# A fused delta-rule and maxout kernel: the first four pieces in program order on every engine, T1's transposes a link later, and half of T read by ScalarE

## The chip, the cores and the metric

The kernel runs on one core of a Trainium2 chip. The metric is the device time of one execution in microseconds (us). Executions of one kernel scatter by about one per cent to either side: the kernel before took from 586.9 to 599.4 us over 39 runs of one series (runs over 1.5% above the fastest of their kernel count as slow, here seven of the 39). So small differences are judged from series of runs taken on the same chip, and with a 95% interval. Profiled executions are single runs with their own span; where two of them are compared, the text says so.

## The reference, cut to what matters

```python
for t in range(S):                       # 4 batches, 8 heads, S = 768, D = 48
    y[:, :, t] = q_t @ state
    v_old = state.T @ k_t                # k normalised
    state = state + beta_t * outer(k_t, v_t - v_old)
x = y.transpose(0, 2, 1, 3).reshape(B * S, H * D)        # 3072 x 384
h = max(x @ w1, x @ w2, x @ w3)                          # 3072 x 768
out = h @ w_out
```

The kernel turns the recurrence into chunks of 64 tokens. For each chunk a triangular system has to be solved; its solution is called T. Then products with T give the updates, and the chunk's outputs go into the maxout block. In the rows below, names with p_ are products on TensorE: p_h is a piece of the maxout block, p_e, p_f, p_z, p_j and p_u are products with T or its parts, p_k, p_q, p_y and p_s those with the state, for the outputs and for the state's update, p_g the grams (products of keys with keys and queries), p_t and p_x transposes. T1 is a part of T that is needed transposed; VectorE transposes it (rows t<-ut).

## The kernel before: the parts that matter

There are six maxout blocks, numbered 0 to 5 here (the recorded texts call them stages, so the second stage is block 1). Block 0 comes in 31 pieces (the first 18 are 256 columns wide and take TensorE some 1.5 us each at full clock), the others in 22 pieces (2.8 us for each of the first 18). Between the pieces, "links" of the recurrence for the next chunks are emitted, so that TensorE (PE) always has dense products to fill in. A piece's product lies in one of two PSUM buffers; ScalarE (ACT) copies the first of three pieces to h, VectorE (DVE) takes the maximum with the two others.

```python
def ps_ffn(shape, name):
    return psum.tile(shape, FP32, name=name, tag="ffn", bufs=2)
...
    if i == 0:
        nc.scalar.copy(h, p_h)
    else:
        nc.vector.tensor_tensor(out=h, in0=h, in1=p_h, op=ALU.max)
    yield
```

The solve runs on DVE in small steps; its result goes through DRAM, as its layout changes on the way:

```python
def solve(m):
    ...                                   # norms, then 15 or 31 steps of two DVE operations
    for half in range(2):
        nc.sync.dma_start(out=y_d[half]..., in_=y[64 * half : 64 * (half + 1)])
    yield
    for cc in range(2):                   # T of the two chunks: ut[0] and ut[1]
        for half in range(2):
            for bb in range(2):
                (one_queue if m or cc else both_queues)[bb].dma_start(out=ut[cc]..., in_=y_d...)
        yield
```

From block 1 on, all engines run in the order of the program. In block 0 only TensorE does; on the other engines a scheduler orders the instructions when the kernel is built, so that, for instance, steps of a solve can be put ahead of copies that come earlier in the program.

## Time and profile before

| | value |
|---|---|
| median of the first series | 595.75 us (594.52 to 596.13, 3 runs) |
| span of the profiled run | 590.0 us |
| TensorE busy | 540.7 us, 92% |
| VectorE, ScalarE, GpSimd busy | 343.5, 140.6, 119.9 us |
| start of blocks 1 to 5 in the profiled run | 195.1, 277.3, 363.8, 447.7, 523.8 us |

How to read it: TensorE is the bound from 135 us on, so anything there that makes TensorE wait is paid in full. Before that, in the head, TensorE is often idle, and the question is what it waits for. The starts of the blocks cut the run into stretches that can be compared between kernels. The lines that carry this are in the prediction.

### The profile page before, as it was taken

Reading aid. Unit: us, or ns where it says so; the run is one execution under the profiler, and the core shown is the slowest. Engines: PE = TensorE matmul, PEld = TensorE weight load, DVE = VectorE, ACT = ScalarE, POOL = GpSimd, SP = SyncE. Lnnn points to the kernel's source line nnn. Section 1 sums busy time; section 2 is a strip of 40 time slices with the busy share of each in tenths; the row PEclk is TensorE's granted clock in tenths of the full one; section 3 lists DMA queues with packets and bytes.
Section 4 is the critical chain, followed back from the end, with each engine's and each line's share of the span. In section 5 each row is a group of like instructions: output and inputs, shape, how many; then the busy total and the mean of one; then the engine's idle time right before and its main releaser. Section 6 shows DMA issues by size and latency. Waiting matters only on the chain.

```text
span 590.0 us, 18726 instructions
## 1 busy us (share of the span) xinstructions
PE 540.7 (92%) x8106; PEld 319.4 (54%) x8106; DVE 343.5 (58%) x778; ACT 140.6 (24%) x274; POOL 119.9 (20%) x209
## 2 busy tenths in 40 slices
PE   5468477979999999999989999999999999999997
PEld 5337365866556555555545555555455455554443
DVE  1658979387499353799643799563997432201110
ACT  3336645345211222111211121220211111010000
POOL 6024535036400323002803003700001000000000
PEclk9555869999999999999989999999999999999999
DMA  9898985556601554264854454843843201210002
GB/s 158 151 177 232 197 160 131 97 151 129 125 21 28 132 117 96 69 122 94 183 120 82 96 96 109 189 101 67 125 102 75 34 2 54 68 40 1 0 0 53
DMA packets 159505, 58.76 MB, mean 100 GB/s; under 512 B 141184, under 2 KB 153280, under 8 KB 159424
## 3 DMA queue, kind: packets, MB, share of 16 engines
q1 hardware_dynamic: 150736, 51.58, 42.4%
q0 software_dynamic: 3200, 4.82, 3.8%
q10 hardware_dynamic: 5488, 1.18, 1.2%
q8 instruction: 63, 1.03, 0.7%
q14 instruction: 18, 0.15, 0.1%
HBM read 40.21 MB, written 17.30 MB: 97 GB/s over the span
## 4 chain that ended last, share of the span: by engine, by line
PE 81%; DVE 5%; DMA 5%; SPq 3%; issue 3%; ACT 2%; POOL 0%; ACTq 0%; DVEq 0%
PE p_h L823 47%; PE p_o L847 16%; PE p_g L411 4%; PE p_k L676 2%; PE p_u L704 2%; PE p_y L744 2%; PE p_s L726 2%; PE p_q L676 2%; DMA kpad<-in_k_dram 2%; PE p_t L339 1%; SPq L369 1%; PE p_j L659 1%; DMA qpad<-in_q_dram 1%; DMA y_d<-y_bl 1%; PE p_z L646 1%
## 5 line engine op out<-in xcount | busy, mean ns | idle before, releaser
L823 PE MATMUL p_h<-xt,w_sb 128*128 128x512 f32 (+1 forms) x702 | 303.0, 577 | 1.4 <-DVE xt L809 1.4
L823 PEld LDWEIGHTS p_h<-xt,w_sb 128*128 128x128 f32 x702 | 130.0, 194 | 123.5 <-issue 113.3
L833 DVE TENSOR_TENSOR h<-h,p_h 128x512 f32<-128x512 f32 (+1 forms) x78 | 50.2, 644 | 102.6 <-PE p_h L823 102.4
L847 PE MATMUL p_o<-wo_sb,h 128*128 128x384 f32 x288 | 94.6, 487 | 0.0
L847 PEld LDWEIGHTS p_o<-wo_sb,h 128*128 128x128 f32 x288 | 54.2, 190 | 37.2 <-issue 1.0
L277 POOL TENSOR_TENSOR v_t<-v_t,nrm 128x768 f32<-128x768 f32 x12 | 17.8, 1479 | 198.1 <-DVE nrm L250 117.1
L523 DVE TENSOR_TENSOR y_bl<-y_bl,tmp 128x31 f32<-128x31 f32 (+20 forms) x139 | 53.4, 384 | 4.6
L369 POOL DMA_DIRECT2D turned<-in_q_dram x96 | 52.4, 553 | 4.1 <-POOL turned L364 3.1
L519 DVE TENSOR_TENSOR tmp<-x_bl,y_bl 128x31 f32<-128x31 f32 (+20 forms) x139 | 47.2, 340 | 4.0
L411 PE MATMUL p_g<-kqt 48*64 48x64 f32 (+1 forms) x1280 | 34.4, 254 | 13.6 <-ACT kqt L345 5.7
L831 ACT COPY h<-p_h 128x512 f32<-128x512 f32 (+1 forms) x39 | 21.5, 552 | 96.4 <-PE p_h L823 96.4
L411 PEld LDWEIGHTS p_g<-kqt 48*64 48x64 f32 x1280 | 28.8, 151 | 22.7 <-issue 10.3
L855 ACT COPY o_sb<-p_o 128x384 f32<-128x384 f32 x24 | 11.5, 478 | 80.7 <-PE p_o L847 72.5
L428 ACT COPY at<-p_g 128x512 f32<-128x512 f32 x21 | 12.3, 586 | 50.0 <-DVE pt L395 40.0
L238 POOL TENSOR_TENSOR w_sb<-mant,up 128x384 int32<-128x384 int32 x18 | 18.5, 1029 | 16.1 <-DVE mant L234 13.6
L732 DVE TENSOR_TENSOR st<-st,p_s 128x768 f32<-128x768 f32 x11 | 10.4, 950 | 17.5 <-PE p_s L726 17.5
L385 DVE STREAM_TRANSPOSE kqt<-turned 128x256 f32<-128x256 f32 x48 | 17.4, 417 | 5.0 <-DMA turned<-in_k_dram 4.8
L696 ACT COPY qs<-p_q 128x768 f32<-128x768 f32 x11 | 8.8, 798 | 47.6 <-DVE v_t L688 27.6
L215 POOL TENSOR_SCALAR mant<-mant 128x384 f32<-128x384 f32 x24 | 12.7, 531 | 36.3 <-ACT mant L211 36.3
L688 DVE TENSOR_TENSOR v_t<-v_t,p_k 128x768 f32<-128x768 f32 x11 | 10.5, 952 | 15.8 <-PE p_k L676 15.8
L395 DVE TENSOR_TENSOR pt<-p_g,mask 128x512 f32<-128x512 f32 x22 | 15.1, 688 | 6.0 <-PE p_g L411 5.7
L676 PEld LDWEIGHTS p_k<-st,kqt 48*64 48x64 f32 x704 | 12.2, 142 | 10.8 <-issue 10.8
(111 smaller groups left out, 494.7 us busy)
## 6 DMA issues: line engine op xcount, KB each, us to landing
w_bits<-in_moe_w_dram SPq DMA_DIRECT2D x18, 384.0 KB
at_d<-at SPq DMA_DIRECT2D x45, 128.0 KB
v_t<-in_v_dram SPq DMA_DIRECT2D x24, 192.0 KB
turned<-in_q_dram POOLq DMA_DIRECT2D x96, 48.0 KB, 3.3
turned<-in_k_dram SPq DMA_DIRECT2D x96, 48.0 KB
out_dram<-o_sb SPq DMA_DIRECT2D x48, 96.0 KB
kpad<-in_k_dram SPq DMA_DIRECT2D x44, 96.0 KB
y_x<-y SPq DMA_DIRECT2D x16, 192.0 KB
```

The lines of the kernel that those rows point to most:

```text
L238: nc.gpsimd.tensor_tensor(out=dst.bitcast(I32), in0=mant_v.bitcast(I32), in1=up_v, op=ALU.add)
L277: nc.gpsimd.tensor_tensor(out=vts[c], in0=vts[c], in1=nrm[:, :, :, None].to_broadcast([128, 2, H, D]), op=ALU.mult,)
L369: (nc.sync, nc.gpsimd)[i].dma_start(out=t[p0 : p0 + 32, bb, at : at + NP * 2 * D].rearrange("p (j x) -> p j x", j=NP), in_=(k, q)[i][2 * b ...
L385: nc.vector.transpose(out=kqts[n][:, :, bb ^ (n % 2), i].rearrange("p j (r tb) -> p j tb r", tb=2), in_=t[:, bb, 32 : 32 + NP * 2 * D].rea ...
L411: nc.tensor.matmul(p_g[rows(bb ^ (g * i)), par, c0 : c0 + C * (1 + whole)], kq[:, 0], kq if whole else kq[:, i],)
L519: nc.vector.tensor_tensor(out=t_v, in0=row.to_broadcast(t_v.shape), in1=column.to_broadcast(t_v.shape), op=ALU.mult,)
L523: nc.vector.tensor_tensor(out=rest, in0=rest, in1=t_v, op=ALU.subtract)
L676: nc.tensor.matmul(p_b[rows(bb), par, c0 : c0 + D], kqt[g][dims(par), j, bb ^ g, i], st[dims(par), bb ^ g, g, j],)
L823: nc.tensor.matmul(p_h, w_sb[i][:, t, f * 128 : (f + 1) * 128], xt[:, t, lo : lo + w], start=(t == 0), stop=(t == KT - 1),)
L831: nc.scalar.copy(h, p_h)
L833: nc.vector.tensor_tensor(out=h, in0=h, in1=p_h, op=ALU.max)
L847: nc.tensor.matmul(p_o, hs[f][:, i * 128 : (i + 1) * 128], wo_sb[:, f], start=(f == 0), stop=(f == FT - 1),)
```

## The change

The intent: let the links of the recurrence in the first pieces of block 0 run undisturbed by conversions of the weights and by the next solve; take T1's transposes off the moment when T arrives; and spare SyncE (SP), which issues nearly all transfers, four of the eight reads of T in each later block.

```diff
+        if m == 0:
+            reads = both_queues, one_queue
+        else:
+            reads = one_queue, one_queue if m < FINE else (nc.scalar, nc.scalar)
...
-                    (one_queue if m or cc else both_queues)[bb].dma_start(
+                    reads[cc][bb].dma_start(
...
-        turn_t1(c)                        # end of halves_u; now emitted by itself:
+    halves_t(0)                           # ahead of the first conversions
+    turn_t1(0)                            # behind halves_u(0)
...
-    by_hand.close()                       # ahead of block 0: every engine in program order ends
-    tc.no_sync_barrier()
...
-        0: "k0 q0 t0 L2", 1: "g0 t1 L3", 2: "g1 d0 d1", 3: "t2", 4: "z0", 5: "z1 g2",
+        0: "k0 q0 t0 L2", 1: "g0 t1 L3", 2: "g1 t2", 3: "d0 d1", 4: "z0", 5: "z1 g2",
... (d1, d0 also enter the links of block 0)
     for i, _ in enumerate(ffn(0)):
-        if i > 2:
+        if i == 4:                        # here: only TensorE from now on
+            by_hand.close()
+            tc.no_sync_barrier()
+            by_hand = ExitStack()
+            by_hand.enter_context(tc.manual_schedule(engines={mybir.EngineType.PE}))
+        if i > 3:
             some(conv, 1)
...
-        if 2 <= i < 9:
-            some(solving, 3)
+        if 4 <= i < 10:
+            some(solving, 4)
```

The ordered part thus holds pieces 0 to 4 and the links behind pieces 0 to 3. In the links, d is T1's transposes, t the transposes of k and q, L the loads for t, g the grams.

## The prediction

> **What bounds the kernel now.** I read the page first: a span of 590.0 us with TensorE (PE) busy for 540.7, so the whole idle of PE is 49.3 us. A cut of the span by stage then shows where it lies. Until the first maxout matmul at 61.36 us, PE is busy 37.5 of 61.4 us; from there to 104.5 us 29.7 of 43.1; to 135 us 27.0 of 30.5; after 135 us, in 455 us, only some 9 us are idle. So this is a PE-bound kernel with a latency-bound head, and the change works on 61 to 135 us (its first four pieces) and, by the read on ScalarE (ACT), on the later stages, where there is nothing idle to win but much to lose.
>
> The windows of 2 us, columns window, length, busy us of PE, weight loads, VectorE (DVE), ACT, GpSimd, then granted clock, DMA share, GB/s:
>
> ```profile
> 64.00:66.00 2.00, 2.00 (x72) 1.87 (x65) 1.84 (x6) 1.85 (x4) 0.52 (x1) 1.00 1.20 165
> 68.00:70.00 2.00, 0.00 (x0) 0.00 (x0) 1.86 (x5) 1.29 (x4) 1.64 (x2) 1.00 0.91 158
> 70.00:72.00 2.00, 0.00 (x0) 0.00 (x0) 1.97 (x5) 1.68 (x6) 1.20 (x2) 0.50 1.19 252
> 80.00:82.00 2.00, 2.00 (x34) 1.88 (x31) 2.00 (x5) 1.08 (x3) 0.51 (x1) 0.50 0.28 35
> 84.00:86.00 2.00, 2.00 (x71) 1.70 (x70) 1.85 (x7) 1.32 (x3) 0.54 (x2) 1.00 0.78 168
> ```
>
> PE stops after piece 1 although DVE works all the time, and the clock stays at a half until some 83 us. The view of waits and the timeline name the cause:
>
> ```profile
> PE p_z L646 <- DVE ut L618: 6.2, 1, 6.2
> ...
> 72.61 0.43 DVE L618 TENSOR_SCALAR ut<-p_f 16x256 f32<-16x256 f32 x1
> 73.18 1.08 PE L646 MATMUL p_z<-ut,at 32*32 32x32 f32 x64 [6.23 <-DVE ut L618]
> ```
>
> The product p_f was done at 63.97 us, but its second negation by DVE ends at 73.04: ahead of it DVE ran conversions, sums and the start of the next solve. That order is the scheduler's, which the change takes away for these pieces.
>
> The later stages, at the start of the third stage's maxout (277.3 us). First SyncE's (SP) queue, then ACT, then PE:
>
> ```profile
> 283.98 1.22 SPq L858 DMA_DIRECT2D out_dram<-o_sb  x2
> 285.30 1.19 SPq L528 DMA_DIRECT2D y_d<-y_bl  x2
> 288.92 5.29 SPq L537 DMA_DIRECT2D ut<-y_d  x8
> 294.31 4.70 SPq L369 DMA_DIRECT2D turned<-in_k_dram  x8
> ...
> 277.57 0.48 ACT L855 COPY o_sb<-p_o 128x384 f32<-128x384 f32 x1 [3.39 <-PE p_o L847]
> 280.10 0.59 ACT L831 COPY h<-p_h 128x512 f32<-128x512 f32 x1 [2.05 <-PE p_h L823]
> ...
> 282.00 2.84 PE L823 MATMUL p_h<-xt,w_sb 128*128 128x512 f32 x6
> ...
> 285.81 2.84 PE L823 MATMUL p_h<-xt,w_sb 128*128 128x512 f32 x6
> ```
>
> The solved T goes to DRAM (y_d) at 285.30 and can be read back only when it has landed, at 288.92: 3.6 us later. PE has by then done three pieces, because ACT copied piece 0 at 280.10.
>
> **What the Trainium skill says.** "TensorE: Matmul & The Clock Gate", What's actually happening: the clock falls to a half after an idle window of about 3.4 us and comes back after about as long busy. This trace agrees: half clock from 70 to 83 us around the stop, and another from 101 to 104 us after an idle of 2.75 us. "DMA: Bandwidth & Descriptors", Issuing engines are not separate DMA queues: issuing from several engines "will only save the time on the sequencer it takes to initiate the DMA". Here that is 5.29 us for eight reads, 0.66 us each. "Perfetto Trace Analysis", DMA Instruction — HWDGE: the wait for semaphores is part of the issuing sequencer's instruction, before the profiled window. So a read that waits holds up all behind it on that engine. This trace shows it for ACT:
>
> ```profile
> 15.89 1.02 ACTq L471 DMA_DIRECT2D x_bl<-at_d  x2
> 16.96 0.94 ACT L296 ACTIVATE ksq<-kpad 128x384 f32<-128x384 f32 x2 [2.68 <-issue]
> ```
>
> ACT's own queue issued two reads when their data had landed (15.75 us in the chain), and the squares behind them, which wait for nothing, began after that.
>
> **The change part by part.**
>
> *First pieces in program order.* DVE's list from piece 0 to piece 4 is now: two negations (0.43 each), the state sum (0.95), maximum (0.42), z (0.69), T1's three transposes (0.45+0.43+0.43), v_t (0.95), mask (0.69), maximum, negation (0.69), mask, maximum: 8.6 us by the durations of the rows. PE's list is five pieces of 1.5, p_f, p_s, p_z, p_k, p_q of about 1.1, two transposes and two grams of 0.66 to 0.7, p_j 0.7: 16 us at full clock. Walking both lists by hand: p_f ends at 63.97, the four negations alternate to about 66.0, piece 1 ends at 66.9, so p_z doesn't wait; v_t ends at 71, the T1 transposes at 70, before p_j at 71.9. I find no stop, so piece 4 ends at about 61.4 + 16 = 77.4 us, instead of 89.3. That is 12 us ahead at that point.
>
> *What it leaves behind.* DVE did 26 us of work in those 28 us; now only 8.6 of it is done. The solve of the second chunk pair starts only behind piece 4: memset 0.95, norms 2.4, 15 steps of about 0.5, that is 10.9 us; beside it five conversions of 0.92 (0.36+0.56), maxima 1.3, y and the state sum 1.9, two masks 1.4. Together 20 us of DVE: the solve ends near 98 us, against 99.0 now. Its T goes to DRAM and back (99.04 to about 110.5 now), then the product p_e may start. PE runs p_e now at 119.20, being late itself; the new PE would be there at 77.4 + 28 = 105 and waits for T until about 110.5. So of 12 us, 8.5 remain. The stops after p_e (2.1 us at 127.35, 0.6 at 123 and 130) stay, as the displaced conversions and norms are there as well.
>
> *No conversion at i = 3, solving in steps of four:* one conversion moves by a piece; the solve needs 19 calls and both versions issue the last at i = 8. Nothing by themselves.
>
> *T1's transposes moved:* DVE's work of 1.33 us for each chunk moves, nothing is added. In the steady stages the k transposes (t2) now go before them.
>
> *T's second half read by ACT* for the stages from the third solve on. Four issues of 0.66 leave SP, 2.6 us, so the k loads behind them (294.31) start earlier. But in program order these four stand behind the last output copy and ahead of piece 0's copy of the next maxout. For three of the four solves (those that end at 282.4, 369.2 and 452.4 us) T has not landed by then. ACT then sits until 288.92, issues four reads (0.35 each on ACT at 39.9 us, so 1.4), and copies piece 0 from about 290.4 to 291.0 instead of at 280.10. PE has two PSUM buffers for pieces: piece 2 (285.81) needs piece 0's, so it starts at 291.1: 5.3 us of idle. The same working for the others: T landed at 375.32, copy done at 377.4, piece 2 wanted at 372.5: 5.0 us. And 455.80, 457.9 against 455.0: 3.0 us. Sum 13.3 us. After idles of that length the half clock costs half of about 3.5 to 5 us each time, an estimate from 101 to 104 and 70 to 83 us here: 2.3 + 2.3 + 1 = 5.5. Against this, PE's two stops for the k transposes (3.5 us in all, at 301.6 and 387.2 us, the first with 1.7 us of half clock behind it) should vanish, as SP is ahead and PE later: 5 us back. The fourth solve (y_d at 191.90) is read at piece 1 of the next maxout and doesn't wait.
>
> *Sum:* -8.5 + 13.3 + 5.5 - 5 = +5.3, so 601 us.
>
> **The rivals.**
> 1. *The read on ACT is harmless*, because T lands before ACT needs its next copy or the two buffers take it up. Then only the head counts: 595.75 - 8.5 - up to 5 for the k transposes, 582 to 587. For it: the change was meant so, and ACT is 24% busy. Against it: 288.92 stands 8.8 us behind 280.10.
> 2. *DVE becomes the bound of the head*: the scheduler again puts the displaced solve and conversions ahead of the copies that PE needs, now behind piece 4. DVE is busy 38.5 of 43.1 us up to 104.5. Then the head gains 2 to 4 us and the whole ends at 605 to 609.
> 3. *The head gains more*, since DVE's conversions and POOL's no longer meet (a 0.3 us operation took 1.1 beside POOL at 90.26 us) and DVE idles 11 of 15 us from 105 to 120. T would come at 106 and the gain be 13: about 596.
>
> **Range and chances.** The head is worth 3 to 13 us, the stages cost 8 to 20 with rival 1 at some 15%. I move my point a little towards a gain for rivals 1 and 3: 599 us, with 586 to 611 holding 8 of 10. Two per cent is 11.9 us: faster needs both rival 1 and a good head (0.10); slower needs rival 2 with the full cost (0.15).
>
> **What would show it.** Right: p_z directly behind piece 1 near 67 us; piece 4 done near 77; p_e near 110; three idles of 3 to 5 us of PE ahead of a maxout piece near 270, 360 and 445 us, put down to ACT's copy, with ACT's own reads of T issued just before it. Wrong: no such idles, PE as dense after 200 us as now; or a stop of over 5 us between 77 and 100 us. If p_e comes as late as now, the head's gain was only moved.

## The result, and the profile after

The changed kernel is correct and slower: median 613.69 us (610.25 to 615.72, 4 runs), against 595.13 us (4 runs) of the kernel before. The ratio is 1.0328 with an interval of 1.0242 to 1.0414. Ratios here are the mean time of one kernel's fast runs over that of the other's of the same rounds, so they aren't quite the ratios of the medians. The prediction, 599 us with 586 to 611, missed.

Where the time came from, from the starts of the blocks in the two profiled runs (the changed kernel's was its slowest of four, and the kernel before's a fast one of 591.78 us, so the differences sum to 24 us instead of some 19):

| stretch | before, us | after, us | difference |
|---|---|---|---|
| to the first piece of block 0 | 61.4 | 63.2 | +1.8 |
| from there to the product p_e of the second pair of chunks | 57.8 | 54.5 | -3.4 |
| from p_e to the start of block 1 | 75.9 | 85.3 | +9.4 |
| block 1 | 82.2 | 82.2 | 0.0 |
| block 2 | 86.4 | 90.0 | +3.6 |
| block 3 | 83.9 | 91.1 | +7.2 |
| block 4 | 76.1 | 81.5 | +5.4 |
| block 5 | 66.2 | 66.2 | 0.0 |

**The later blocks** went as foretold. TensorE's waits after 200 us are one single line in the view of waits (engine, product, what it waited for, us in total, times, longest):

```profile
PE p_h L826 <- ACT h L834: 15.2, 3, 5.9
```

At the start of block 2, ACT's timeline shows the four reads, then the copy of piece 0, and TensorE's timeline the third piece:

```profile
296.93 2.00 ACTq L541 DMA_DIRECT2D ut<-y_d  x4
298.97 0.58 ACT L834 COPY h<-p_h 128x512 f32<-128x512 f32 x1 [13.10 <-DMA ut<-y_d]
...
299.61 4.72 PE L826 MATMUL p_h<-xt,w_sb 128*128 128x512 f32 x6 [5.91 <-ACT h L834]
```

ACT stood for 13.1 us at a read of data that wasn't there. The copy behind it came at 298.97 instead of some 288 us, so TensorE had no PSUM buffer for its third piece and stood 5.91 us. The piece itself then took 4.72 us where 2.84 is usual: the granted clock was 0.50 from 296.7 to 303.4 us.

**The head** went another way. In windows from 63 to 84, 84 to 118 and 118 to 150 us (columns as in the prediction: PE, weight loads, DVE, ACT, GpSimd, clock, DMA), first of the kernel before:

```profile
63.00:84.00 21.00, 11.38 (x308) 9.65 (x304) 17.58 (x41) 10.72 (x25) 10.40 (x14) 0.67 0.96 171
84.00:118.00 34.00, 30.04 (x673) 24.98 (x673) 23.64 (x59) 16.11 (x30) 10.38 (x12) 0.95 0.58 124
118.00:150.00 32.00, 27.84 (x734) 20.57 (x732) 24.55 (x51) 15.13 (x31) 17.49 (x29) 0.95 0.62 139
```

and of the changed kernel:

```profile
63.00:84.00 21.00, 18.63 (x486) 15.36 (x486) 9.04 (x16) 6.08 (x13) 2.12 (x3) 0.80 0.50 106
84.00:118.00 34.00, 26.85 (x539) 21.91 (x538) 29.72 (x76) 20.03 (x40) 15.26 (x19) 0.95 0.65 135
118.00:150.00 32.00, 24.97 (x620) 20.51 (x621) 27.91 (x55) 15.31 (x32) 16.95 (x24) 0.78 0.61 152
```

In the ordered pieces TensorE is far better off (18.6 us busy instead of 11.4). But DVE does only 9.0 us of work there instead of 17.6; it then has to make up for it, is busy for 29.7 of 34 us, and is still behind after 118 us, where TensorE loses what it had won and the clock falls to 0.78. SP's queue shows what that means for T, first before, then after:

```profile
86.61 2.67 SPq L273 DMA_DIRECT2D ksum<-kflip  x2
...
99.04 1.15 SPq L528 DMA_DIRECT2D y_d<-wo_sb  x2
```

```profile
111.03 1.13 SPq L528 DMA_DIRECT2D y_d<-wo_sb  x2
...
118.98 1.90 SPq L273 DMA_DIRECT2D ksum<-kflip  x2
```

T is written 12 us later. The small exchanges of sums (ksum), from which the norms of the next chunks come, moved from ahead of it to behind it, 32 us later. TensorE pays for the late T at the product p_e, and for the late sums at the product p_f; in the kernel before neither wait is there:

```profile
PE p_e L615 <- DMA ut<-y_d: 3.9, 2, 3.6
PE p_f L632 <- DVE v_t L691: 3.6, 1, 3.6
```

### The profile page after: what moved, and what is told of

It reads as the page before. It is cut to its first block, busy times and chain, and to the rows that moved or that the text cites. A ratio compares the mean times of both kernels' runs of the same rounds, so it can differ in the third digit from the quotient of the medians.

```text
span 614.0 us, 18720 instructions
## 1 busy us (share of the span) xinstructions
PE 552.2 (90%) x8106; PEld 324.1 (53%) x8106; DVE 344.4 (56%) x778; ACT 140.0 (23%) x274; POOL 121.0 (20%) x209
## 4 chain that ended last, share of the span: by engine, by line
PE 52%; DVE 17%; DMA 14%; SPq 9%; issue 4%; ACT 2%; ACTq 1%; POOL 1%; DVEq 0%; POOLq 0%
PE p_h L826 33%; PE p_o L850 7%; DMA kpad<-in_k_dram 5%; DVE y_bl L523 3%; DVE tmp L519 3%; DMA y_x<-y 3%; PE p_g L411 3%; SPq L115 3%; DMA y_d<-y_bl 3%; SPq L369 1%; PE p_j L662 1%; DVE y L749 1%; SPq L788 1%; DMA w_bits<-in_moe_w_dram 1%; PE p_t L339 1%
## 5 line engine op out<-in xcount | busy, mean ns | idle before, releaser
L826 PE MATMUL p_h<-xt,w_sb 128*128 128x512 f32 (+1 forms) x702 | 312.1, 591 | 16.5 <-ACT h L834 15.2
L826 PEld LDWEIGHTS p_h<-xt,w_sb 128*128 128x128 f32 x702 | 133.4, 199 | 143.0 <-issue 115.3
L523 DVE TENSOR_TENSOR y_bl<-y_bl,tmp 128x31 f32<-128x31 f32 (+20 forms) x139 | 54.5, 392 | 4.7
L858 ACT COPY o_sb<-p_o 128x384 f32<-128x384 f32 x24 | 11.5, 478 | 82.2 <-PE p_o L850 74.9
L238 POOL TENSOR_TENSOR w_sb<-mant,up 128x384 int32<-128x384 int32 x18 | 18.6, 1033 | 21.8 <-DVE mant L234 16.0
L622 DVE TENSOR_SCALAR ut<-p_j 32x512 f32<-32x512 f32 (+1 forms) x13 | 8.3, 647 | 19.5 <-ACT ut L624 19.5
L364 POOL MEMSET turned<- 128x96 f32 x24 | 4.0, 186 | 72.2 <-DVE kqt L385 72.2
L707 PEld LDWEIGHTS p_u<-v_t,ut 64*64 64x64 f32 x768 | 13.4, 142 | 7.7 <-issue 7.4
```

The source lines that it names most:

```text
L238: nc.gpsimd.tensor_tensor(out=dst.bitcast(I32), in0=mant_v.bitcast(I32), in1=up_v, op=ALU.add)
L523: nc.vector.tensor_tensor(out=rest, in0=rest, in1=t_v, op=ALU.subtract)
L707: nc.tensor.matmul(p_v[rows(bb ^ g), g, i], ut[c % NU][rows(bb), g, h], rhs[rows(bb), g, h],)
L826: nc.tensor.matmul(p_h, w_sb[i][:, t, f * 128 : (f + 1) * 128], xt[:, t, lo : lo + w], start=(t == 0), stop=(t == KT - 1),)
```

## The experiments

Fourteen kernels ran. Of the kernels with only a part of the change, the diffs are against the changed kernel if they say so, else against the kernel before.

**1. The read on ScalarE alone.**

```diff
- (one_queue if m or cc else both_queues)[bb].dma_start(
+ (both_queues if not (m or cc) else (nc.scalar, nc.scalar) if cc and m >= FINE else one_queue)[bb].dma_start(
```

> The kernel before with one part of the change alone: from the third solve on, the second half of T is read by ScalarE. Theory (ScalarE stands at the read until T has landed, so TensorE runs out of PSUM buffers at the third piece of three maxout stages): three idles of TensorE of 5.3, 5.0 and 3.0 us put down to ScalarE's copy of h, and the part of the trace after the head 12 to 17 us longer, so 607 to 613 us in all, with the head up to the second stage as before (195 us). Rival (the read on ScalarE costs nothing by itself, and the stops come from the head being late): 592 to 597 us.

Measured: 607.59 us median, ratio 1.0239 (1.0180 to 1.0297), so about 14 us more. The view of waits of its later blocks again has a single line:

```profile
PE p_h L823 <- ACT h L831: 16.1, 3, 6.6
```

Block 1 starts at 196.1 us, within 1 us of before; blocks 2, 3 and 4 are 4.1, 7.8 and 5.3 us longer in the profiled run, the slowest of its four. So this part alone is most of the loss, and it needs none of the others. The rival falls.

**2. The change without the read on ScalarE** (against the changed kernel).

```diff
-            reads = one_queue, one_queue if m < FINE else (nc.scalar, nc.scalar)
+            reads = one_queue, one_queue
```

> The changed kernel with the read on ScalarE taken back to SyncE; all the rest of the change stays. Theory (the two parts are independent, and the head costs some 7 us): second stage begins near 203 us instead of 195, no idle put down to the copy of h, 598 to 603 us in all. Rival (the head gains as predicted, and what the trace shows of it is one bad execution): second stage near 187 us, 584 to 589 us.

Measured: 601.55 us median (598.54 to 606.25, 4 runs), ratio 1.0156 (1.0075 to 1.0236). Block 1 starts at 199.0 us, 4 us late rather than 8. No wait for ACT's copy is left. But blocks 2 and 3 are 1.7 and 1.2 us longer than before, which neither theory had said. The next runs look at that.

**3. The solve put off, with the scheduler free from piece 0** (against the run just told).

```diff
+    by_hand.close(); tc.no_sync_barrier()       # ahead of block 0, as in the kernel before
+    by_hand = ...                               # only TensorE in program order
     for i, _ in enumerate(ffn(0)):
-        if i == 4: ...                          # the same four lines
```

> As the changed kernel without the read on ScalarE, but the scheduler has all engines except TensorE free from piece 0, as in the kernel before; so the solve and the conversions are put off by a piece or two, and nothing is in program order. If the putting off of the solve is what costs the head, this costs as much as with the order: 600 us or more. If the order of the first four pieces costs it, this is as before: 593 to 597 us.

Measured: 600.12 us, ratio 1.0107 (1.0047 to 1.0166). By the time alone the first guess would be confirmed, but the trace says otherwise: T is written at 99.25 us and block 1 starts at 195.5 us, as before. A scheduler that is free brings the steps forward, whatever piece they are emitted at. The loss lies in blocks 2 and 3, 2.9 and 3.2 us longer. What is left of the change there is the move of T1's transposes.

**4. Program order, without putting off the solve** (against experiment 2).

```diff
-        if i > 3:
+        if i > 2:
             some(conv, 1)
-        if 4 <= i < 10:
-            some(solving, 4)
+        if 2 <= i < 9:
+            some(solving, 3)
```

> As the changed kernel without the read on ScalarE, with the first pieces in program order on every engine, but the solve in steps of three from piece 2 and the conversions from piece 3 as in the kernel before. If the putting off of the solve costs the head, its solve ends some 5 us sooner than in the changed kernel (105 us instead of 111), T is read sooner, and the whole takes 590 to 596 us. If VectorE's total of work in the head is what counts, wherever it stands, it stays at 598 to 603 us.

Measured: 604.75 us, ratio 1.0189 (1.0131 to 1.0247); T is written at 106.8 us, block 1 starts at 201.1 us. Six solve steps and a conversion inside the ordered pieces bring T 3 us forward (it was written at 110.1 us in experiment 2), but no time. So with the order kept, undoing this much of the putting off wins nothing. That the order costs whatever DVE does in it isn't shown by this: experiment 10 moves the whole solve.

**5. T1's moves alone** (the changed kernel with the read, the order, the conversions and the solve as before).

> The kernel before with the moves of T1's transposes alone (in the head and, in the steady stages, one link later, so behind the k transposes t2). Theory: the k transposes wait some 9 us for a late k load, and T1's transposes, whose data is there, now stand behind them on VectorE; two steady stages get 2 to 3 us longer each, so 597 to 601 us, with the head as before (second stage at 195 us). Rival (it costs nothing, the order of the head does): 593 to 596 us.

Measured: 603.13 us (601.11 to 605.92, 4 runs), ratio 1.0160 (1.0074 to 1.0246). The head is as before within the scatter (block 1 at 198.0 us; the kernels with the old head have 195.1 to 198.0). Blocks 2 and 3 are 2.9 and 5.0 us longer. DVE's timeline in block 2:

```profile
300.48 0.45 DVE L385 STREAM_TRANSPOSE kqt<-turned 128x256 f32<-128x256 f32 x1 [7.13 <-DMA turned<-in_k_dram]
303.14 1.10 DVE L385 STREAM_TRANSPOSE kqt<-turned 128x256 f32<-128x256 f32 x3 [2.21 <-DMA turned<-in_k_dram]
304.16 0.40 DVE L573 STREAM_TRANSPOSE t<-ut 128x256 f32<-128x256 f32 x1
```

DVE waits 7.1 and 2.2 us for a load of k, and only then does T1's transposes, whose data has been there for some time. They take 2.7 us for both chunks, in front of the maxima that TensorE waits for (4.4 us in the view of waits, two stops of 2.2 us). Before, they ran inside that wait. The stops are only half of it: the two pieces behind them took 5.49 and 5.32 us instead of 2.84, at a granted clock of 0.50, which is 5.1 us more. So a move that adds no work cost 8 us in two blocks of this profile.

**6. Only the head changed** (against the changed kernel: the read on SP, and T1's transposes in the links of blocks 1 to 5 where they were).

> The changed kernel without the read on ScalarE and with T1's transposes in the steady stages where they were; so only the head is changed. Theory (program order leaves VectorE idle for 12 of 21 us in the first pieces, and what it did not do there delays the solve, the writing of T and with it the SyncE queue): second stage 4 to 8 us late, the later stages as before, 598 to 602 us. Rival (the head costs nothing and all of the earlier run's loss was T1's): 593 to 597 us.

Measured: 599.04 us median over 20 runs, 12 of them fast, ratio of the fast runs 1.0074 (1.0042 to 1.0106), 4.4 us more. Seven of the eight slow ones show clocks of 0.930 to 0.936, which also occur in the fast runs of experiment 2 (0.925 to 0.939), so the line at 1.5% may only cut off the upper end of the scatter; over all runs the means differ by 5.9 us. The profiled run, at a clock of 0.90, isn't used for times. The four other ordered heads of the fast runs (experiments 2, 4, 9 and 11) start block 1 at 198.4 to 201.1 us, the changed kernel itself at 203.0.

**7. The ordered head filled with the solve, first attempt** (against experiment 6).

```diff
-        if 4 <= i < 10:
-            some(solving, 4)
+        if i < 4:
+            some(solving, 5)
```

> As the run with only the head changed, but the solve runs in the ordered pieces, five steps in each of pieces 0 to 3, so that VectorE's idle time there is filled. Theory: VectorE is busy some 19 of 21 to 24 us in these pieces, T is written near 85 to 90 us instead of 110, the SyncE queue isn't held up, the second stage begins at 188 to 196 us, 586 to 596 us in all. Rival (the head is bound by loads, or by the chain after the product with T): the second stage stays near 200 us, 598 us or more.

The result was wrong (relative error 0.19), by my mistake: the twenty steps include the loads of the new T, and these then stood in the program ahead of the product that still reads the old T. Its 605.74 us say nothing about the theory. That product waited 10.5 us for the loads.

**8. The read on ScalarE two pieces later.** The solve stops after the reads of the first half; the second half's follow behind piece 2 of the next block.

```diff
-            if i < 2:
+            if i == 2 or (m == 1 and i == 0):
                 some(solving, 1)
...
-            if i >= 11:
+            if 11 <= i < 21:
                 some(solving, 2)
```

and the line of experiment 1.

> The kernel before with the second half of T read by ScalarE, but two pieces later, when T has landed; nothing else. Theory (what hurts is only where the read stands in ScalarE's program): no idle put down to the copy of h; the k loads start some 2.5 us earlier, so the stops of 2.3 and 1.2 us before the grams vanish: 589 to 594 us. Rival (a read issued by ScalarE costs by itself, or the k loads aren't held by SyncE's issues): 595 us or more, with these stops as before.

Measured: 590.08 us median over 20 runs (all fast), ratio 0.9938 (0.9915 to 0.9960). This is faster than the kernel before, by 3.7 us, the fastest of all that ran. ACT's timeline in block 2 shows why:

```profile
282.91 0.58 ACT L831 COPY h<-p_h 128x512 f32<-128x512 f32 x1 [2.05 <-PE p_h L823]
...
289.48 0.58 ACT L428 COPY at<-p_g 128x512 f32<-128x512 f32 x1 [3.73 <-DVE pt L395]
291.68 2.86 ACTq L537 DMA_DIRECT2D ut<-y_d  x4
294.59 0.58 ACT L428 COPY at<-p_g 128x512 f32<-128x512 f32 x1 [4.52 <-DMA ut<-y_d]
```

The copy of piece 0 (282.91) now stands ahead of the read. ACT still waits, but 4.5 us and not 13, and TensorE does not notice. TensorE's waits after 200 us:

```profile
PE p_g L411 <- DVE kqt L385: 1.1, 1, 1.1
PE p_z L646 <- DMA ut<-y_d: 0.9, 2, 0.7
```

They were 3.5 us for the grams, whose loads of k SP now issues 15.5 us after the start of block 2 instead of 17.0. Block 2 is 2.9 us shorter than before. The same four reads on the same queue cost 14 us at one place of the program and win 4 at another.

**9. The changed kernel with the read two pieces later** (the two edits of the loop from experiment 8, on the changed kernel).

> The changed kernel with one thing changed: the second half of T is read by ScalarE two pieces later. Theory (where the read stands is the largest part of the loss): no idle put down to the copy of h, 13 to 17 us less than the changed kernel, so 597 to 602 us; the head stays 4 to 8 us late, and a cost of T1's late transposes, up to 4 us, may show again. Rival: it stays over 606 us.

Measured: 600.18 us, ratio 1.0104 (1.0072 to 1.0137). Against the changed kernel's 613.69, of another series, that is 13.5 us. Here TensorE's waits for DVE's maxima are back, 4.2 us in two waits: with ACT's stop gone, T1's late transposes show.

**10. The filled head, mended** (against experiment 6; the solve and the writing of T in pieces 0 to 3, the last loads behind the product at piece 4).

```diff
-        if 4 <= i < 10:
-            some(solving, 4)
+        if i < 5:
+            some(solving, (5, 5, 5, 3, 1)[i])
```

> The filled head again, mended: in the run before, the loads of the second pair's T were put ahead of the product that still reads the old T, which made the result wrong and put a wait of 10.5 us there. Now the solve and the writing of T stand in pieces 0 to 3 and the last load behind that product. Theory (in program order VectorE's idle time in the first pieces is what the head loses, and it can be used): T is written near 89 us, no wait of several us for T, the second stage begins at 188 to 196 us, 585 to 595 us in all. Rival (the head is bound by what comes after: conversions, norms, loads of k, or the wait moves to another of them): 597 us or more, second stage at 199 us or later.

Measured: correct, 593.70 us over 20 runs, ratio 1.0020 (0.9991 to 1.0049). Program order with DVE filled costs nothing that these runs could separate; some three of the 4.4 us are back. The two series ran on different chips and their intervals overlap a little, so this is shown narrowly; experiment 12 supports it. But T is written at 88.6 us, 10 us before the time of the kernel before, and nothing is won by that. The windows of the profiled run, which at 596.89 us was slower than the median:

```profile
63.00:84.00 21.00, 17.09 (x430) 13.75 (x432) 15.44 (x43) 5.12 (x12) 2.46 (x3) 0.71 0.46 98
84.00:118.00 34.00, 27.82 (x573) 23.21 (x564) 22.76 (x48) 18.91 (x36) 12.43 (x17) 0.90 0.75 149
118.00:150.00 32.00, 26.00 (x662) 20.26 (x661) 27.08 (x58) 16.73 (x35) 17.95 (x25) 0.84 0.55 142
```

DVE did 15.4 us in the ordered pieces, in the next stretch about as much as in the kernel before (22.8 us), and after 118 us was nearly as loaded as in the changed kernel. TensorE waited 4.6 us for ACT's copy of u (the product p_y) and 3.8 us for v_t. So the theory holds for the loss and not for the gain. The traces say more of the gain. ACT and TensorE:

```profile
91.78 0.56 ACT L211 ACTIVATE mant<-w_bits 128x384 f32<-128x384 f32 x1 [4.25 <-POOL w_sb L238]
...
94.02 1.96 PE L747 MATMUL p_y<-u,pt 64*64 64x48 f32 x64 [4.64 <-ACT u L712]
...
119.00 1.09 PE L615 MATMUL p_e<-ut,at 64*64 64x32 f32 x64
```

The copy of u stands on ACT behind a step of a conversion, which waits for GpSimd (POOL) and so for DVE's part of an earlier conversion, which DVE ran behind the solve. And p_e, the first product with the new T, starts at 119.0 us without a wait; in the kernel before it started at 119.2, also without one. So an earlier T can't bring p_e forward by itself: TensorE's own list ahead of it has to get done sooner, and that lost 4.6 us at p_y.

**11. The changed kernel with T1's transposes where they were in the later blocks.**

```diff
- 2: "g1 t2", 3: "d0 d1",
+ 2: "g1 d0 d1", 3: "t2",
```

> The changed kernel with one thing undone: in the steady stages T1's transposes stand where they were. Alone their move cost some 8 us in the stages. Theory: beside ScalarE's early read that cost is hidden, as TensorE stands for ScalarE anyway and the k loads are early; so 609 to 616 us, as the changed kernel. Rival (the costs add): 603 to 608 us.

Measured: 611.93 us, ratio 1.0294 (1.0255 to 1.0333), which isn't separable from the changed kernel's 1.0328. So beside ACT's early read T1's move is hidden, as expected.

**12. The filled head and the late read together.**

> The filled head together with the read on ScalarE two pieces later. If the two gains add, this is the fastest of all, 580 to 591 us; if the filled head brings nothing, it is 3 to 4 us under the filled head alone.

Measured: 591.16 us over 16 runs, ratio 0.9958 (0.9937 to 0.9979). The gain is that of the late read (0.9938), within their intervals. The wait of 4.6 us for u at p_y is here too.

**13. Only the head, with early sums** (against experiment 6).

```diff
-        if i in (8, 9):
-            prep(i - 6)
+        if i in (2, 3):
+            prep_sums(i)
+        if i in (5, 6):
+            prep_values(i - 3)
```

> As the run with only the head changed, but the sums of squares of the next two chunks, and with them the small exchanges of sums that SyncE issues, are emitted at pieces 2 and 3 and the norms at 5 and 6, instead of both at 8 and 9. Theory (in the ordered head these exchanges come at 116 to 119 us on the SyncE queue, behind the writing of T, where the kernel before had them at 87 to 93; v_t and then TensorE wait 3.6 us for the norms, and a half clock follows): exchanges near 80 to 95 us, the wait for v_t gone, the second stage 3 to 5 us earlier than in that run, 593 to 597 us in all. Rival (the solve's late end alone sets the head): no more than 1 us is won, 598 to 600 us.

Measured: 601.29 us, ratio 1.0145 (1.0108 to 1.0182). A miss: the exchanges of sums came at 82.4 us and the wait for v_t was gone, as expected, yet it is slower than without. T is written at 115.4 us, DVE is busy for 32.2 of the 34 us from 84 to 118, and TensorE waits in other places (2.7 us for u, 2.3 us for xt, 1.8 us at p_f). The wait had only moved.

**14. All three remedies.**

> All three remedies together: solve in the ordered pieces, early sums, and the read on ScalarE two pieces later. If the waits that are left in the filled head (3.8 us for v_t, 4.6 us for u) are the norms' and a queue's order, the first goes: 584 to 589 us. If the wait only moves: 590 to 592 us, as without the early sums.

Measured: 596.82 us, ratio 1.0081 (1.0049 to 1.0113). Again the wait moved: v_t's is gone, and ACT's copy of u came so late that TensorE stood for 9.9 us before p_y. In ACT's timeline a square root stands four rows ahead of that copy and waits 6.1 us for the exchange of sums to land. This is the fault of experiment 1 once more: an engine with a copy to do, behind an instruction that waits for a transfer.

## Why the prediction was wrong

Step by step, as it was put:

- *ACT's read in the later blocks*: right in mechanism and nearly in size. Three idles of 5.3, 5.0 and 3.0 us were worked out; 5.9, 5.9 and 3.4 came. The four issues on ACT took 2.0 us, not 1.4. With the clock and the vanished stops for the k transposes the blocks were to cost 13.8 us; the profiled run shows 16.2 (3.6 + 7.2 + 5.4), the kernel with this part alone 14 us by its ratio (17.2 in its profiled run). Experiments 1, 8 and 9 show that it is the place of the read in ACT's program.
- *T1's transposes moved: "nothing is added"*: right that no work is added, wrong that it therefore costs nothing. Alone it costs about 8 us in blocks 2 and 3 of the profiled run. In the changed kernel this is hidden behind ACT's read (experiment 11); that the sum wasn't hurt by it was luck.
- *"No stop, so piece 4 ends at 77.4"*: it ended at 84.1. Piece 0 began 1.8 us later; the granted clock was 0.50 for the first 4.7 us and again from 74.8 to 78.1, which the walk had left out; and TensorE stood 2.2 us at p_k for a reason that the profile doesn't show ("issue"), as it had for 3.0 us before.
- *"The solve ends near 98 us"*, which is the step that failed. It ended at 111.0, 13 us later: 6.7 of them because piece 4 was late, the others because DVE had 26.1 us to do from there and not 20. Rows of DVE overlap a little; counted each from its start to the next row's, these 26.1 us are 11.6 for the solve and 0.9 for a memset (10.9 expected for both), 7.5 for conversions, which were eight and not five (4.6 expected; some were stretched beside GpSimd), 1.9 for four sums of squares that I had left out, and 4.2 for the rest (4.6 expected). The memset is not that solve's but one of a later solve, put forward.
- *"Of 12 us, 8.5 remain"*: p_e came at 117.7, not 110.5, so 1.5 us were left.
- *"The stops after p_e stay"*: they grew. From p_e to block 1 the profiled run took 9.4 us more, with 3.6 us for v_t among them, and a half clock behind them.

So rival 2, that DVE becomes the bound of the head behind piece 4, was what happened, and a little worse than I had put it: the head lost 4 us (experiment 6) where the rival still let it gain 2 to 4. I had seen that the change leaves most of DVE's work in the first 28 us of the head undone, and then spread it over a stretch which I took to have room. (The 26 us in the prediction are a sum of overlapping rows; the view of windows gives 23.9 busy from 61.36 to 89.30. The list of 8.6 us adds up to 8.1.) It had little: DVE was busy 23.6 of 34 us there already. The largest stops were not those for copies, which rival 2 had named (1.8 us for kqt at the grams), but the late T (3.9 us) and v_t (3.6 us). Had the head's term been +4.4 instead of -8.5, the sum would have been 614 us, near the 613.69 measured; the agreement is partly chance, as the costs of T1's move and of ACT's read don't add.

Two things stay open. What holds the filled head (experiment 10) at the time of the kernel before, though T comes 10 us sooner, was read from the traces, the conversion ahead of the copy of u, but no run tested it; taking away the wait for v_t moved it elsewhere. And the "issue" stop at p_k, 1.1 to 3.8 us in 14 of the 16 profiles and absent in those of experiments 2 and 11, was not explained.

## What to carry to other kernels

Before a transfer's issue is given to an engine that also computes, find out when the data it waits for lands, and what the engine has to do next: the wait holds up everything behind it on that engine, and the engines that it feeds stand as soon as their buffers are used up. Before an order is imposed on a stretch, count for every engine how much work of later parts it did in the stretch's gaps, since that work comes back as a load on what follows. And moving an instruction behind one that waits can cost time, even if no work is added.

## What the Trainium skill lacked or had wrong

- "DMA: Bandwidth & Descriptors", Issuing engines are not separate DMA queues, says that issuing from several engines only saves the sequencer's time for the issue. On ACT, which also has copies to do, it is not only that: the same four reads cost 14 us where they stood ahead of a due copy with the data not yet landed (ACT stood 13.1 us, TensorE 5.9), and won 3.7 us two pieces later. That the wait for semaphores lies within the issuing sequencer, which is free for the next instruction only after it, is in "Perfetto Trace Analysis", DMA Instruction — HWDGE; that the engine's own copies behind the read wait with it, and what that can cost, is spelt out in neither place.
- "TensorE: Matmul & The Clock Gate", What's actually happening, gives an idle window of about 3.4 us before the clock falls to a half. Shorter idles were enough here: in the kernel before, the granted clock was 0.50 from 100.8 to 104.0 us after an idle of 2.75 us, and from 302.2 to 305.4 after one of 2.32 us. (The prediction called the first of these agreement.) After the stop of 5.91 us in the changed kernel the piece of six matmuls took 4.72 us instead of 2.84, so that stop cost 1.9 us on top of 5.9.
- "SBUF — State Buffer", SBUF: two separate sides, says that a DVE operation with two SBUF inputs and a GpSimd operation that reads SBUF exclude each other for the whole instruction. The trace agrees: a DVE product of 0.28 us took 1.10 us at 90.26 us in the kernel before, beside a GpSimd addition from 89.96 to 91.21 us. No page says how to count this in a sum of rows.
- No page says that a scheduler's free order may be worth more than a hand-made order. Here four pieces in program order left DVE with 9.0 us of work in 21 us where it had done 17.6, and cost 4.4 us in all.
